# Linear attention on one core: the denominator moved into the four column groups of TensorE and spread afterwards

## The chip, the cores and the metric

One core of one Trainium2 chip runs the whole program. The metric is the device time of one execution in microseconds. A profile is one more execution, taken by the hardware profiler. Its "span" is about 1.7 us shorter than the time of the same execution.

## The reference, cut to what matters

```python
B, S, D = 1, 2048, 640;  H = 32; Dh = 20          # bf16 inputs
q, k, v = split_heads(x @ wqkv)
phi = lambda t: where(t > 0, t + 1, exp(t)) + 1e-6
pq, pk = phi(q), phi(k)
kv  = einsum("bhsd,bhse->bhde", pk, v)
z   = einsum("bhsd->bhd", pk)
num = einsum("bhqd,bhde->bhqe", pq, kv)
den = einsum("bhqd,bhd->bhq", pq, z)[..., None] + 1e-6   # one number per row and head
out = (num / den) merged over heads @ wo
```

There are only 32 denominators for each of the 2048 rows, but each divides 20 features.

## The kernel before

The kernel keeps `pq` transposed: 128 feature rows by 512 sequence rows, five such pieces (`c`) for each of four row blocks (`sbk`). The 128 feature rows of a piece are 32 heads times 4 features. Since `kv` and `wo` are folded into one matrix (`w2p`), the kernel divides `pq` by the denominator before the output matmul. The denominator therefore has to stand on all 128 feature rows. The kernel before gets this straight from TensorE: its weight block `zb` is 128 wide and repeats each head's column four times.

```python
def den(sbk, b):
    def mm(e):
        for c in range(NC_):                       # 5 matmuls of 128x512
            r = e.matmul(bank(b), zb[:, 128 * c:128 * c + 128],
                         pq[:, c * S + BK * sbk:c * S + BK * (sbk + 1)],
                         start=(c == 0), stop=(c == NC_ - 1))
        return r
    P.add("pe", mm, ...)
    i = sbk % 2
    P.add("act", lambda e: e.activation(lb[i], bank(b), ACTF.Ln, bias=eps[:, 0:1]), ...)
    P.add("act", lambda e: e.activation(rd[i], lb[i], ACTF.Exp, scale=-1.0), ...)   # 1/den

def normalize(sbk):                                # VectorE: pq *= rd, 5 times 128x512
    ...

# ... (program order of the second half; q = make one Q tile in the PSUM bank named)
den(0, 4); next_q(7); w2_group(2, 2); next_q(5); w2_group(3, 0); normalize(0)
next_q(6); w2_group(4, 2); next_q(7); w2_group(5, 0)
den(1, 4); w2_rows(); next_q(5); next_q(6); normalize(1)
while qi[0] < 15:
    next_q((7, 2, 3, 5, 6)[qi[0] % 5])             # one Q tile, the 15th: bank 6
next_q(0); next_q(1); den(2, 4)
next_q(2); normalize(2); next_q(3); next_q(5)
for st in range(2): out_tile(st)                   # output tile st uses banks 2*(st%4), +1
den(3, 6); normalize(3)
for st in range(2, NT): out_tile(st)
```

A Q tile is five 128x512 matmuls, an Exp on ScalarE (`eq`), and two operations on VectorE (`eq`, then `pq`, which is the last to read the bank). Each engine has its own list of instructions and waits on semaphores for the others.

Of the kernel before, what the change touches and what calls it, by code (L numbers as in the profile page):

```python
# [6 lines left out]
ACTF = mybir.ActivationFunctionType  # L7
ALU = mybir.AluOpType
BF16 = mybir.dt.bfloat16
F32 = mybir.dt.float32  # L10
# [72 lines left out]
def bass_standalone__linear_attn_block__prompt_kernel(nc, x, wqkv, wo, out):  # L83
    B, S, D = x.shape
    assert (B, S, D) == (1, 2048, 640)
    H, DH = 32, 20
    NC_ = D // 128
    NT = S // 128
    HALF = D // 2
    NSB = S // 512  # L90
    GW, NG = 120, 6
    gsz = [min(GW, D - GW * g) for g in range(NG)]
    BK = 512

    with contextlib.ExitStack() as ctx:
        es = ctx.enter_context

        def sb(name, cols, dt=BF16):
            return es(nc.sbuf_tensor(name, [128, cols], dt))
# [10 lines left out]
        pq = sb("pq", NC_ * S)  # L110
# [5 lines left out]
        za = [sb(f"za{j}", 2 * D, F32) for j in range(4)]  # L116
        zs = sb("zs", D, F32)
        zc = sb("zc", 8, F32)
        zb = sb("zb", NC_ * 128)
        hm = sb("hm", 128)  # L120
        bm = sb("bm", GW)
        ones = sb("ones", 8, F32)
        eps = sb("eps", 8, F32)
        zero = sb("zero", BK)
        lb = [sb(f"lb{j}", BK, F32) for j in range(2)]
        rd = [sb(f"rd{j}", BK) for j in range(2)]
        osb = [sb(f"osb{j}", D) for j in range(4)]
        ps = es(nc.psum_tensor("ps", [128, 8 * BK], F32))
        w2d = nc.dram_tensor("w2_rows", (D, D), BF16, kind="Internal").ap()

        P = Plan(nc, es)

        def bank(b, n=BK, off=0, parts=128):
            return ps[0:parts, BK * b + off:BK * b + off + n]
# [5 lines left out]
        def fold(ap, j=HALF):  # L140
            return ap.rearrange("p (g j) -> p g j", j=j)


        def pool_const():
            P.add("dve", lambda e: e.memset(zero[:, :], 0.0), writes=["zero"])
            P.add("dve", lambda e: e.memset(ones[:, :], 1.0), writes=["ones"])
            P.add("dve", lambda e: e.memset(eps[:, :], 1e-6), writes=["eps"])  # L147
            P.add("pool", lambda e: e.memset(wv[:, NC_ * D:], 0.0), writes=["wvpad"])
            P.add("pool", lambda e: e.memset(hm[:, :], 1.0), writes=["hm"])
            P.add("pool", lambda e: e.memset(bm[:, :], 1.0), writes=["bm"])  # L150
            for t, w, name in ((hm, 4, "hm"), (bm, DH, "bm")):
                n = t.shape[1] // w
                for lo in (True, False):
                    P.add("pool", lambda e, t=t, w=w, n=n, lo=lo: e.affine_select(
                        out=t[:, :].rearrange("p (a b) -> p a b", b=w),
                        in_=t[:, :].rearrange("p (a b) -> p a b", b=w),
                        pattern=[[-w if lo else w, n], [0, w]],
                        base=0 if lo else w - 1,
                        channel_multiplier=1 if lo else -1,
                        compare_op=ALU.is_ge, fill=0.0), reads=[name], writes=[name])  # L160

        XCH = [(0, 256), (256, 512), (512, 1024), (1024, 1536), (1536, 2048)]

# [158 lines left out]
        def z_finish(b):  # L322
            def mm(e):
                for c in range(NC_):
                    r = e.matmul(bank(b, 1, off=c), zs[:, 128 * c:128 * c + 128],
                                 ones[:, 0:1], start=True, stop=True)
                return r
            P.add("pe", mm, reads=["zs", "ones"], writes=[("bank", b)])
            P.add("dve", lambda e: e.tensor_copy(zc[:, 0:NC_], bank(b, NC_)),
                  reads=[("bank", b)], writes=["zc"])  # L330
            for c in range(NC_):
                P.add("dve", lambda e, c=c: e.tensor_scalar(
                    zb[:, 128 * c:128 * c + 128], hm[:, :], zc[:, c:c + 1], None, ALU.mult),
                    reads=["hm", "zc"], writes=[("zb", c)])

        def kv_group(b):
# [25 lines left out]
        def w2_group(g, b):  # L362
            n = gsz[g]
            for h in range(2):
                P.add("pe", lambda e, h=h: e.matmul(  # L365
                    bank(b + h, HALF, parts=n), kvt[0:n, GW * g:GW * g + n],
                    wog[0:n, g * D + HALF * h:g * D + HALF * (h + 1)], start=True, stop=True),
                    reads=[("kvt", 0 if g < 4 else g - 3), "wog", "wog5"],
                    writes=[("bank", b + h)])
            P.add("act", lambda e: e.copy(  # L370
                fold(w2g[0:n, g * D:(g + 1) * D]), two_banks(b, parts=n)),
                reads=[("bank", b), ("bank", b + 1)], writes=[("w2g", g)])

        def w2_rows():
            P.add("sp", lambda e: e.dma_start(
                w2d[0:5 * GW, :].rearrange("(g p) n -> p g n", p=GW),
                w2g[0:GW, 0:5 * D].rearrange("p (g n) -> p g n", n=D)),
                reads=[("w2g", g) for g in range(5)], writes=["w2d"], dma=True)
            P.add("sp", lambda e: e.dma_start(
                w2d[5 * GW:D, :], w2g[0:gsz[5], 5 * D:6 * D]),  # L380
                reads=[("w2g", 5)], writes=["w2d5"], dma=True)
            for c in range(NC_):
                P.add("sp", lambda e, c=c: e.dma_start(
                    w2p[:, c * D:(c + 1) * D],
                    w2d.rearrange("(h c j) n -> c h j n", c=NC_, j=4)[c]),
                    reads=["w2d", "w2d5"], writes=[("w2p", c)], dma=True)

        def den(sbk, b):
            def mm(e):
                for c in range(NC_):  # L390
                    r = e.matmul(bank(b), zb[:, 128 * c:128 * c + 128],  # L391
                                 pq[:, c * S + BK * sbk:c * S + BK * (sbk + 1)],
                                 start=(c == 0), stop=(c == NC_ - 1))
                return r
            P.add("pe", mm, reads=[("zb", c) for c in range(NC_)]
                  + [("pq", sbk, c) for c in range(NC_)], writes=[("bank", b)])
            i = sbk % 2
            P.add("act", lambda e: e.activation(lb[i][:, :], bank(b), ACTF.Ln, bias=eps[:, 0:1]),  # L398
                  reads=[("bank", b), "eps", "table"], writes=[("lb", i)])
            P.add("act", lambda e: e.activation(rd[i][:, :], lb[i][:, :], ACTF.Exp, scale=-1.0),  # L400
                  reads=[("lb", i)], writes=[("rd", i)])

        def normalize(sbk):
            i = sbk % 2
            for c in range(NC_):
                v = pq[:, c * S + BK * sbk:c * S + BK * (sbk + 1)]
                P.add("dve", lambda e, v=v: e.tensor_tensor(v, v, rd[i][:, :], ALU.mult),  # L407
                      reads=[("rd", i), ("pq", sbk, c)], writes=[("pq", sbk, c)])

        def out_tile(st):  # L410
            b = 2 * (st % 4)
            j = st % 4
            for h in range(2):
                def mm(e, h=h):
                    for c in range(NC_):
                        r = e.matmul(bank(b + h, HALF),  # L416
                                     pq[:, c * S + 128 * st:c * S + 128 * st + 128],
                                     w2p[:, c * D + HALF * h:c * D + HALF * (h + 1)],
                                     start=(c == 0), stop=(c == NC_ - 1))
                    return r  # L420
                P.add("pe", mm, reads=[("pq", st // 4, c) for c in range(NC_)]
                      + [("w2p", c) for c in range(NC_)], writes=[("bank", b + h)])
            P.add("act", lambda e: e.copy(osb[j][:, 0:HALF], bank(b, HALF)),  # L423
                  reads=[("bank", b)], writes=[("osb", j, 0)])
            P.add("dve", lambda e: e.tensor_copy(osb[j][:, HALF:D], bank(b + 1, HALF)),  # L425
                  reads=[("bank", b + 1)], writes=[("osb", j, 1)])
            P.add("sp", lambda e: e.dma_start(
                out[0, 128 * st:128 * st + 128, :], osb[j][:, :]),
                reads=[("osb", j, 0), ("osb", j, 1)], writes=[("out", st)], dma=True)
# [14 lines left out]
        def next_q(b):  # L444
            q_tile(*qs[qi[0]], b)
            qi[0] += 1
# [17 lines left out]
        next_q(6)  # L464
        w2_group(1, 0)
        den(0, 4)
        next_q(7)
        w2_group(2, 2)
        next_q(5)
        w2_group(3, 0)  # L470
        normalize(0)
# [3 lines left out]
        w2_group(5, 0)  # L475
        den(1, 4)
        w2_rows()
        next_q(5)
        next_q(6)
        normalize(1)  # L480
        while qi[0] < 15:
            next_q((7, 2, 3, 5, 6)[qi[0] % 5])
        next_q(0)
        next_q(1)
        den(2, 4)
        next_q(2)
        normalize(2)
        next_q(3)
        next_q(5)
        for st in range(2):  # L490
            out_tile(st)
        den(3, 6)
        normalize(3)
        for st in range(2, NT):
            out_tile(st)

        block = es(nc.Block())
# [51 lines left out]
```

## Time and profile before

| | before |
|---|---|
| time, median | 111.83 us |
| TensorE busy | 101.5 of 110.1 us |
| denominator matmuls | 4 x 5, 216 ns apart: 1.08 us a block |
| Ln and Exp of a block | 688 and 630 ns |
| waits of TensorE after 58 us | 1.75, 0.31 and about 0.25 us (the last worked out from starts, as a record is missing there) |

First the page: engine totals with shares of the span and instruction counts, the granted clock in 40 slices (9 is 90% or more), and the shares of the chain of waits by engine.

```profile
PE 101.5 (92%) x662; PEld 64.0 (58%) x668; DVE 66.9 (61%) x132; ACT 41.9 (38%) x73; POOL 5.9 (5%) x16
...
PEclk9999999999999999999999999999999999999999
...
PE 70%; DVE 15%; DMA 6%; ACT 5%; issue 1%
```

TensorE is busy for 92% of the span and makes 70% of the chain. So its matmul time counts, wherever it is not waiting. The groups view says what one instruction costs (count, then busy us and mean ns of one, then idle before it):

```profile
L391 PE MATMUL ps<-pq,zb 128*128 128x512 bf16 x19 | 4.8, 380 | 0.4 <-DVE pq L288 0.3
L398 ACT ACTIVATE lb<-ps,eps 128x512 f32<-128x512 f32 x4 | 2.8, 688 | 3.4 <-PE ps L391 3.4
L400 ACT ACTIVATE rd<-lb 128x512 bf16<-128x512 f32 x4 | 2.5, 630 | 0.1
L344 PE MATMUL ps<-pt,wv 128*40 128x40 bf16 x5 | 0.3, 182 | 0.0
```

A mean of 380 ns is the life of one matmul, not its price: the next one starts after 216 ns. One of the 20 denominator records is missing. TensorE's timeline in order of time shows the prices (start us, length us, line, count; a length runs from the first start to the last end):

```profile
64.21 1.25 PE L391 MATMUL ps<-pq,zb 128*128 128x512 bf16 x5
65.30 1.24 PE L275 MATMUL ps<-xT,wqp 128*128 128x512 bf16 x5
66.38 0.44 PE L365 MATMUL ps<-wog,kvt 120*120 120x320 bf16 x2
66.66 1.24 PE L275 MATMUL ps<-xT,wqp 128*128 128x512 bf16 x5
...
70.92 1.25 PE L391 MATMUL ps<-pq,zb 128*128 128x512 bf16 x5
72.00 2.32 PE L275 MATMUL ps<-xT,wqp 128*128 128x512 bf16 x9
76.08 3.41 PE L275 MATMUL ps<-xT,wqp 128*128 128x512 bf16 x15 [1.75 <-DVE pq L288]
79.33 1.24 PE L391 MATMUL ps<-pq,zb 128*128 128x512 bf16 x5
80.40 3.40 PE L275 MATMUL ps<-xT,wqp 128*128 128x512 bf16 x15
...
87.30 1.03 PE L391 MATMUL ps<-pq,zb 128*128 128x512 bf16 x4 [0.30 <-DVE pq L288]
88.17 8.04 PE L416 MATMUL ps<-w2p,pq 128*128 128x320 bf16 x58
```

From a block's first matmul to the next group's first are 1.07 to 1.09 us: that is what TensorE pays for a denominator. The record missing is the first of the last block, which therefore began at about 87.08 (87.30 less 0.216).

### The profile page before, as it was taken

What the parts mean: (1) busy time and instruction counts of PE and PEld (TensorE: products, weight loads), DVE (VectorE), ACT (ScalarE), POOL (GpSimd) and SP (SyncE); (2) the same over time, 40 slices, a digit from 0 to 9 for tenths busy, and PEclk for the clock granted to TensorE, in tenths of its full rate; (3) what the DMA queues carried; (4) which work ended last, traced back from release to release, by engine and by line L of the source; (5) the groups of instructions that cost most, each with busy time, mean ns of one, the idle gap of its engine ahead of it and who ended that gap; (6) DMA issues with size and microseconds to landing.
All of it is one profiled execution on the core that took longest, in us unless ns stands there. A gap on an engine that the chain in (4) does not pass through costs nothing.

```text
span 110.1 us, 1693 instructions
## 1 busy us (share of the span) xinstructions
PE 101.5 (92%) x662; PEld 64.0 (58%) x668; DVE 66.9 (61%) x132; ACT 41.9 (38%) x73; POOL 5.9 (5%) x16
## 2 busy tenths in 40 slices
PE   5969999999799999999999999993999799999990
PEld 2327777777477674676757745431446377777760
DVE  1004888998899899701137664969849837333331
ACT  3104555555500206202043379872575173333330
POOL 7100000750000000000000000000000000000000
PEclk9999999999999999999999999999999999999999
DMA  1999999999980000000000000082720032433333
GB/s 40 270 295 220 224 211 298 378 363 364 258 163 22 0 0 3 0 0 0 6 0 3 0 0 0 18 216 70 206 92 0 0 119 92 152 119 119 119 120 118
DMA packets 19497, 12.88 MB, mean 117 GB/s; under 512 B 10914, under 2 KB 19490, under 8 KB 19490
## 3 DMA queue, kind: packets, MB, share of 16 engines
q1 hardware_dynamic: 18178, 11.96, 39.4%
q10 hardware_dynamic: 1312, 0.82, 2.7%
q8 instruction: 5, 0.08, 0.3%
q14 instruction: 2, 0.02, 0.0%
HBM read 6.72 MB, written 3.44 MB: 92 GB/s over the span
## 4 chain that ended last, share of the span: by engine, by line
PE 70%; DVE 15%; DMA 6%; ACT 5%; issue 1%
PE ps L225 19%; PE ps L416 17%; PE ps L249 15%; PE ps L275 12%; DMA xT<-in_x_dram 6%; DVE pq L288 4%; PE ps L391 4%; DVE za L294 4%; ACT eq L283 2%; DVE eq L285 2%; DVE pq L407 2%; PE ps L344 1%; ACT lb L398 1%; PE ps L365 1%; ACT rd L400 1%
## 5 line engine op out<-in xcount | busy, mean ns | idle before, releaser
L275 PE MATMUL ps<-xT,wqp 128*128 128x512 bf16 x95 | 23.0, 379 | 2.0 <-DVE pq L288 1.8
L249 PE MATMUL ps<-pk,xn 128*128 128x320 bf16 x160 | 22.4, 299 | 0.8 <-DVE pk L240 0.7
L225 PE MATMUL ps<-wk,xT 128*128 128x320 bf16 x160 | 21.9, 299 | 1.1 <-DMA xT<-in_x_dram 1.1
L416 PE MATMUL ps<-w2p,pq 128*128 128x320 bf16 x160 | 22.2, 299 | 0.3 <-DVE pq L288 0.3
L249 PEld LDWEIGHTS ps<-pk,xn 128*128 128x128 bf16 x160 | 15.5, 98 | 7.9 <-DVE pk L240 1.0
L225 PEld LDWEIGHTS ps<-wk,xT 128*128 128x128 bf16 x160 | 15.6, 98 | 7.5 <-issue 1.5
L283 ACT ACTIVATE eq<-ps 128x512 bf16<-128x512 f32 x20 | 11.9, 595 | 21.2 <-PE ps L275 20.7
L416 PEld LDWEIGHTS ps<-w2p,pq 128*128 128x128 bf16 x160 | 15.6, 98 | 7.0 <-DVE pq L288 0.6
L235 ACT ACTIVATE ek<-ps 128x640 bf16<-128x640 f32 x16 | 11.3, 704 | 15.7 <-PE ps L225 15.7
L275 PEld LDWEIGHTS ps<-xT,wqp 128*128 128x128 bf16 x100 | 9.6, 98 | 12.2 <-DVE pq L288 2.2
L288 DVE SCALAR_TENSOR_TENSOR pq<-ps,eq 128x512 bf16<-128x512 f32 x20 | 13.8, 692 | 0.7
L285 DVE TENSOR_SCALAR eq<-eq 128x512 bf16<-128x512 bf16 x20 | 5.8, 290 | 12.8 <-ACT eq L283 12.6
L240 DVE SCALAR_TENSOR_TENSOR pk<-ps,ek 128x640 bf16<-128x640 f32 x16 | 13.2, 824 | 0.6
L425 DVE CAST osb<-ps 128x320 bf16<-128x320 f32 x16 | 7.7, 489 | 9.6 <-PE ps L416 9.5
L237 DVE TENSOR_SCALAR ek<-ek 128x640 bf16<-128x640 bf16 x16 | 6.1, 380 | 10.5 <-ACT ek L235 10.4
L423 ACT CAST osb<-ps 128x320 bf16<-128x320 f32 x16 | 6.8, 425 | 12.6 <-PE ps L416 12.5
L407 DVE TENSOR_TENSOR pq<-pq,rd 128x512 bf16<-128x512 bf16 x20 | 7.0, 417 | 2.0 <-ACT rd L400 2.0
L216 PE MATMUL ps<-zero 128*128 128x512 bf16 x16 | 5.2, 494 | 1.3 <-DVE eps L147 1.3
L261 ACT CAST pt<-ps 128x320 bf16<-128x320 f32 x6 | 2.2, 434 | 9.7 <-PE ps L249 9.7
L294 DVE TENSOR_TENSOR za<-pk 128x1280 f32<-128x1280 bf16 x4 | 5.7, 1483 | 0.0
L391 PE MATMUL ps<-pq,zb 128*128 128x512 bf16 x19 | 4.8, 380 | 0.4 <-DVE pq L288 0.3
L208 POOL COPY wqp<-wqn 128x640 bf16<-128x640 bf16 x5 | 3.6, 756 | 16.9 <-DMA wqn<-in_wqkv_dram 16.9
(30 smaller groups left out, 36.1 us busy)
## 6 DMA issues: line engine op xcount, KB each, us to landing
xn<-in_x_dram SPq DMA_DIRECT2D x4, 640.0 KB, 9.7
out_dram<-osb SPq DMA_DIRECT2D x16, 160.0 KB, 1.8
wk<-in_wqkv_dram ACTq DMA_DIRECT2D x2, 400.0 KB, 5.0
wqn<-in_wqkv_dram SPq DMA_DIRECT2D x1, 800.0 KB, 5.2
wv<-in_wqkv_dram SPq DMA_DIRECT2D x1, 800.0 KB, 14.3
w2p<-w_rows SPq DMA_DIRECT2D x5, 160.0 KB, 2.7
wog<-in_wo_dram SPq DMA_DIRECT2D x1, 750.0 KB, 14.8
w_rows<-w2g SPq DMA_DIRECT2D x1, 750.0 KB, 5.3
```

Source lines behind the costliest of these rows:

```text
L225: r = e.matmul(bank(b + h, HALF), xT[:, c * S + 128 * st:c * S + 128 * st + 128], wk[:, c * D + HALF * h:c * D + HALF * (h + 1)], start=(c ...
L235: P.add("act", lambda e: e.activation(fold(t[:, :]), two_banks(b), ACTF.Exp), reads=banks + ["table"], writes=[("ek", st % 3)])
L240: P.add("dve", lambda e: e.scalar_tensor_tensor(fold(pk[:, st * D:(st + 1) * D]), two_banks(b), 0.0, fold(t[:, :]), ALU.max, ALU.add), rea ...
L249: r = e.matmul(bank(d, HALF), xn[:, st * D + 128 * d:st * D + 128 * d + 128], pk[:, st * D + HALF * h:st * D + HALF * (h + 1)], start=(st ...
L275: r = e.matmul(bank(b), wqp[:, d * D + 128 * c:d * D + 128 * c + 128], xT[:, d * S + BK * sbk:d * S + BK * (sbk + 1)], start=(d == 0), sto ...
L283: P.add("act", lambda e: e.activation(t[:, :], bank(b), ACTF.Exp), reads=[("bank", b), "table"], writes=[("eq", i)])
L285: P.add("dve", lambda e: e.tensor_scalar(t[:, :], t[:, :], 1.0, 1e-6, ALU.min, ALU.add), reads=[("eq", i)], writes=[("eq", i)])
L288: P.add("dve", lambda e: e.scalar_tensor_tensor(pq[:, c * S + BK * sbk:c * S + BK * (sbk + 1)], bank(b), 0.0, t[:, :], ALU.max, ALU.add), ...
L294: P.add("dve", lambda e: e.tensor_tensor(d_ap, a, b, ALU.add), reads=ra + rb, writes=[dst])
L391: r = e.matmul(bank(b), zb[:, 128 * c:128 * c + 128], pq[:, c * S + BK * sbk:c * S + BK * (sbk + 1)], start=(c == 0), stop=(c == NC_ - 1))
L407: P.add("dve", lambda e, v=v: e.tensor_tensor(v, v, rd[i][:, :], ALU.mult), reads=[("rd", i), ("pq", sbk, c)], writes=[("pq", sbk, c)])
L416: r = e.matmul(bank(b + h, HALF), pq[:, c * S + 128 * st:c * S + 128 * st + 128], w2p[:, c * D + HALF * h:c * D + HALF * (h + 1)], start=( ...
```

## The change

Its intent: compute each denominator once, not four times. The weights `zb` become 32 wide. The 512 rows of a block are cut into four pieces of 128, and each piece goes to its own column group of the array (output partitions 0-31, 32-63, 64-95, 96-127), so that the four can run side by side. The sums then fill 128 partitions by 128 columns, a quarter of the columns for Ln and Exp. Four matmuls with a 0/1 mask `em` spread the inverse to the 128 feature rows, and ScalarE copies the result to `rd`.

```diff
-        zb = sb("zb", NC_ * 128)
-        hm = sb("hm", 128)
+        zb = sb("zb", NC_ * 32)
+        em = sb("em", 4 * 128)          # four 0/1 masks, made by GpSimd at the start
+        hm = sb("hm", 32)
 ... (building of the masks cut)
         def den(sbk, b):
             def mm(e):
                 for c in range(NC_):
-                    r = e.matmul(bank(b), zb[:, 128 * c:128 * c + 128],
-                                 pq[:, c * S + BK * sbk:c * S + BK * (sbk + 1)],
-                                 start=(c == 0), stop=(c == NC_ - 1))
+                    for k in range(4):
+                        r = e.matmul(
+                            ps[32 * k:32 * k + 32, BK * b:BK * b + 128],
+                            zb[:, 32 * c:32 * c + 32],
+                            pq[:, c * S + BK * sbk + 128 * k:c * S + BK * sbk + 128 * k + 128],
+                            start=(c == 0), stop=(c == NC_ - 1))
                 return r
+        def den_act(sbk, b):              # Ln and Exp on 128 columns -> rdc
+            ...
+        def den_spread(sbk, b):
+            def mm(e):
+                for k in range(4):
+                    r = e.matmul(bank(b, 128, off=128 * k), em[:, 128 * k:128 * k + 128],
+                                 rdc[i][:, :], start=True, stop=True)
+                return r
+            P.add("pe", mm, reads=["em", ("rdc", i)], writes=[("bank", b)])
+            P.add("act", lambda e: e.copy(rd[i][:, :], bank(b)), ...)
 ... (order: each den is followed by den_act; den_spread comes one or two tiles later)
         den(2, 4)
+        den_act(2, 4)
         next_q(2)
+        next_q(3)
+        den_spread(2, 4)
         normalize(2)
-        next_q(3)
         next_q(5)
         for st in range(2):
             out_tile(st)
         den(3, 6)
+        den_act(3, 6)
+        out_tile(2)
+        den_spread(3, 6)
         normalize(3)
-        for st in range(2, NT):
+        for st in range(3, NT):
             out_tile(st)
```

More of the change, by code (lines that the diff above doesn't have):

```diff
@@ L124, in bass_standalone__linear_attn_block__prompt_kernel @@
         zero = sb("zero", BK)
-        lb = [sb(f"lb{j}", BK, F32) for j in range(2)]
+        lb = [sb(f"lb{j}", 128, F32) for j in range(2)]
+        rdc = [sb(f"rdc{j}", 128) for j in range(2)]
         rd = [sb(f"rd{j}", BK) for j in range(2)]
@@ L150, in pool_const, with band @@
             P.add("pool", lambda e: e.memset(bm[:, :], 1.0), writes=["bm"])
-            for t, w, name in ((hm, 4, "hm"), (bm, DH, "bm")):
-                n = t.shape[1] // w
-                for lo in (True, False):
-                    P.add("pool", lambda e, t=t, w=w, n=n, lo=lo: e.affine_select(
-                        out=t[:, :].rearrange("p (a b) -> p a b", b=w),
-                        in_=t[:, :].rearrange("p (a b) -> p a b", b=w),
-                        pattern=[[-w if lo else w, n], [0, w]],
-                        base=0 if lo else w - 1,
-                        channel_multiplier=1 if lo else -1,
-                        compare_op=ALU.is_ge, fill=0.0), reads=[name], writes=[name])
+            P.add("pool", lambda e: e.memset(em[:, :], 1.0), writes=["em"])
+            def band(t, pat, base, mult, name):
+                v = t.rearrange("p (a b) -> p a b", b=pat[1][1])
+                P.add("pool", lambda e: e.affine_select(
+                    out=v, in_=v, pattern=pat, base=base, channel_multiplier=mult,
+                    compare_op=ALU.is_ge, fill=0.0), reads=[name], writes=[name])
+            band(hm[:, :], [[-4, 32], [0, 1]], 0, 1, "hm")
+            band(hm[:, :], [[4, 32], [0, 1]], 3, -1, "hm")
+            for k in range(4):
+                m = em[:, 128 * k:128 * k + 128]
+                band(m, [[-1, 32], [0, 4]], -32 * k, 1, "em")
+                band(m, [[1, 32], [0, 4]], 32 * k, -1, "em")
+            for lo in (True, False):
+                band(bm[:, :], [[-DH if lo else DH, NG], [0, DH]],
+                     0 if lo else DH - 1, 1 if lo else -1, "bm")
         XCH = [(0, 256), (256, 512), (512, 1024), (1024, 1536), (1536, 2048)]
@@ L332, in z_finish @@
                 P.add("dve", lambda e, c=c: e.tensor_scalar(
-                    zb[:, 128 * c:128 * c + 128], hm[:, :], zc[:, c:c + 1], None, ALU.mult),
+                    zb[:, 32 * c:32 * c + 32], hm[:, :], zc[:, c:c + 1], None, ALU.mult),
                     reads=["hm", "zc"], writes=[("zb", c)])
@@ L396, in den @@
                   + [("pq", sbk, c) for c in range(NC_)], writes=[("bank", b)])
+        def den_act(sbk, b):
             i = sbk % 2
-            P.add("act", lambda e: e.activation(lb[i][:, :], bank(b), ACTF.Ln, bias=eps[:, 0:1]),
+            P.add("act", lambda e: e.activation(lb[i][:, :], bank(b, 128), ACTF.Ln, bias=eps[:, 0:1]),
                   reads=[("bank", b), "eps", "table"], writes=[("lb", i)])
-            P.add("act", lambda e: e.activation(rd[i][:, :], lb[i][:, :], ACTF.Exp, scale=-1.0),
-                  reads=[("lb", i)], writes=[("rd", i)])
+            P.add("act", lambda e: e.activation(rdc[i][:, :], lb[i][:, :], ACTF.Exp, scale=-1.0),
+                  reads=[("lb", i)], writes=[("rdc", i)])
+        def den_spread(sbk, b):
+            i = sbk % 2
+            def mm(e):
+                for k in range(4):
+                    r = e.matmul(bank(b, 128, off=128 * k), em[:, 128 * k:128 * k + 128],
+                                 rdc[i][:, :], start=True, stop=True)
+                return r
+            P.add("pe", mm, reads=["em", ("rdc", i)], writes=[("bank", b)])
+            P.add("act", lambda e: e.copy(rd[i][:, :], bank(b)),
+                  reads=[("bank", b)], writes=[("rd", i)])
         def normalize(sbk):
@@ L466, in bass_standalone__linear_attn_block__prompt_kernel @@
         den(0, 4)
+        den_act(0, 4)
         next_q(7)
         w2_group(2, 2)
+        den_spread(0, 4)
         next_q(5)
@@ L477, in bass_standalone__linear_attn_block__prompt_kernel @@
         w2_rows()
+        den_act(1, 4)
         next_q(5)
         next_q(6)
+        den_spread(1, 4)
         normalize(1)
```

## The prediction

> **What bounds it now.** TensorE: 101.5 of 110.1 us busy (page, engine totals), full clock in every slice, and 70% of the chain of waits. The denominator matmuls are 4% of that chain. In the chain's time order four blocks of five 128x512 matmuls take 1.25, 1.20, 1.09 and about 1.25 us (87.07 to 88.33, one record missing); 216 ns each, about 1.08 us streaming. TensorE really waits at only three places from 58 us on (its timeline): 1.75 us before 76.08 (a Q tile reuses the bank of the Q tile before, so it waits for ScalarE and VectorE), 0.31 before 86.15 and about 0.25 before 87.07 (both for VectorE's pq).
>
> **Removed.** 20 streams of 512 columns become 80 of 128 in four column groups. Groups view: 128x40 weight-plus-matmul pairs of the kv step follow each other at about 30 ns (five span 0.30, one lasts 0.18), 128x120 ones at 53 ns. So a block is 20 x 30 = 0.6 us if the groups overlap and issue limits, 20 x 53 = 1.06 us if they don't. The Trainium skill ("TensorE: Matmul & The Clock Gate", What's actually happening) gives about 25 ns as the smallest start-to-start, which fits the 30 ns here. I take 0.75 us: 0.33 saved per block, 1.3 us in all.
>
> **Added by the tile mode.** The skill ("TensorEngine Tiling (Array Packing)", Key Properties) says that changing tiling mode drains TensorE. In this trace the 40*40 matmuls start 0.31 us after the last 512-column one (216 ns usual) and the next full matmul 0.23 us after the last of them (136 usual): about 0.09 us per switch. Seven exposed switches: 0.6 us.
>
> **ScalarE saves nothing.** Ln 688 and Exp 630 ns at 512 columns shrink to about 360 and 310 (slope 0.85 ns per column, from Exp at 512 and 640 columns: 595 and 704), but a 512-column copy of about 600 ns is added.
>
> **Spread.** Four 128-column matmuls, 0.21 us a block. Block 0: on TensorE's critical stretch, +0.2. Block 1: falls into the 1.75 us wait, free. Block 2: free, because VectorE decides when denominator 3 may start (Q tiles 17, 18, 19 and the normalize: about 6.4 us after denominator 2 in both orders). Block 3: +0.2 and a new wait: it writes bank 6, which output tile 3 needs next, so TensorE waits for the spread's completion and the 0.6 us copy: about +0.8 us. Nothing else is there for it to do.
>
> **Small.** The five zb products on 32 columns instead of 128 shorten a wait of at most 0.2 us: -0.1. The masks add some 4 us to GpSimd at the start, where it idles 17 us: free.
>
> **Sum.** -1.3 + 0.6 + 0.2 + 0.2 + 0.8 - 0.1 = +0.4 us. Predicted 112.2 us, range 111.2 to 113.9. Chances: faster by over 2% 0.02, within 2% 0.90, slower by over 2% 0.08.
>
> **What would show it.** Denominator block: first to last start plus one, 0.6 to 0.9 us. Full matmul after it about 0.1 us late. TensorE idle of 0.7 to 0.9 us before output tile 3, ended by ScalarE's rd copy. The wait before the 15th Q tile stays, ended by VectorE pq, a little shorter. Denominator 3 still released by VectorE pq. Output stage still about 136 ns per matmul.
>
> **What would make it wrong.** Column groups that don't overlap, or weight loads of 32 columns that aren't hidden behind them: a block of 1.1 us or more, +1.3 us or more in all. Switches that cost nothing: -0.6. A later VectorE order that frees den 3 sooner. The spread finding its inverse not ready (I expect over 0.4 us of slack everywhere).

One reference in it needs a correction: the figure of 25 ns stands on the page named, but in the section after the one named, "Wait — 56ns, not 53.3ns?".

## The result, and the profile after

The changed kernel takes 110.52 us (median of 4, 110.34 to 110.94); the kernel before in the same rounds takes 111.82. The ratio is 0.9886, interval 0.9854 to 0.9919. The change gains 1.3 us where I had forecast a loss of 0.4; the time lies below the range I gave.

The page after, the same lines as before:

```profile
PE 100.1 (92%) x738; PEld 64.2 (59%) x744; DVE 66.7 (61%) x132; ACT 41.4 (38%) x77; POOL 10.2 (9%) x25
...
PE 72%; DVE 13%; DMA 6%; ACT 5%; issue 1%
```

TensorE lost 1.4 us of busy time although it has 76 more matmul records. The groups view after:

```profile
L405 PE MATMUL ps<-pq,zb 128*32 128x128 bf16 x80 | 1.9, 221 | 0.3 <-DVE pq L300 0.3
L416 ACT ACTIVATE lb<-ps,eps 128x128 f32<-128x128 f32 x4 | 1.5, 370 | 1.1 <-PE ps L405 1.1
L418 ACT ACTIVATE rdc<-lb 128x128 bf16<-128x128 f32 x4 | 1.2, 310 | 0.1
L430 ACT CAST rd<-ps 128x512 bf16<-128x512 f32 x4 | 2.3, 587 | 0.5 <-PE ps L426 0.5
```

And TensorE's timeline after:

```profile
64.64 0.46 PE L405 MATMUL ps<-pq,zb 128*32 128x128 bf16 x20
65.04 1.25 PE L287 MATMUL ps<-xT,wqp 128*128 128x512 bf16 x5
66.13 0.44 PE L377 MATMUL ps<-wog,kvt 120*120 120x320 bf16 x2
66.40 0.39 PE L426 MATMUL ps<-rdc,em 128*128 128x128 bf16 x4
66.62 1.24 PE L287 MATMUL ps<-xT,wqp 128*128 128x512 bf16 x5
...
70.88 0.46 PE L405 MATMUL ps<-pq,zb 128*32 128x128 bf16 x20
71.28 2.33 PE L287 MATMUL ps<-xT,wqp 128*128 128x512 bf16 x10
...
75.36 3.41 PE L287 MATMUL ps<-xT,wqp 128*128 128x512 bf16 x14 [1.52 <-DVE pq L300]
78.70 0.46 PE L405 MATMUL ps<-pq,zb 128*32 128x128 bf16 x20
79.09 2.33 PE L287 MATMUL ps<-xT,wqp 128*128 128x512 bf16 x10
...
85.77 0.46 PE L405 MATMUL ps<-pq,zb 128*32 128x128 bf16 x20 [0.32 <-DVE pq L300]
86.16 1.53 PE L446 MATMUL ps<-w2p,pq 128*128 128x320 bf16 x10
87.53 0.39 PE L426 MATMUL ps<-rdc,em 128*128 128x128 bf16 x4
88.59 7.64 PE L446 MATMUL ps<-w2p,pq 128*128 128x320 bf16 x55 [0.68 <-ACT rd L430]
```

A block of 20 narrow matmuls lasts 0.46 us, of which the last matmul's own life is 0.22: first to last start are 0.24 us, 12.6 ns per matmul on average. The next matmul starts 0.39 to 0.40 us after the block's first. Before it was 1.08.

Putting the same milestones of the two traces side by side gives a ledger. "Step" is by how much the difference changes from one line to the next.

| TensorE starts | before | after | difference | step, and what it is |
|---|---|---|---|---|
| first k matmul | 7.49 | 8.04 | +0.55 | load of x in this execution |
| denominator 0 | 64.21 | 64.64 | +0.43 | -0.12, shorter zb products |
| Q tile after it | 65.30 | 65.04 | -0.26 | -0.69, denominator 0 |
| Q tile after spread 0 | 66.66 | 66.62 | -0.04 | +0.22, spread 0 |
| Q tile after denominator 1 | 72.00 | 71.28 | -0.72 | -0.68, denominator 1 |
| 15th Q tile | 76.08 | 75.36 | -0.72 | 0, spread 1 |
| Q tile after denominator 2 | 80.40 | 79.09 | -1.31 | -0.59, denominator 2 |
| denominator 3 | 87.08 | 85.77 | -1.31 | 0, spread 2 |
| output tile 2 | 88.17 | 86.16 | -2.01 | -0.70, denominator 3 |
| output tile 3 | 89.53 | 88.59 | -0.94 | +1.07, spread 3 and its wait |

(Output tile 3 before is worked out: ten matmuls of 136 ns after output tile 2.) Leaving out the first line, which is a longer load of x in the profiled execution (the slowest of its four, 110.94 us), the change gains 1.5 us: the four denominator blocks give 2.66, the zb products 0.12, and spreads 0 and 3 take back 1.29. The load was issued at 0.81 us in both traces and took 7.09 us against 6.55. It does not come with the change: in the nine other traces of kernels with the changed denominator the first k matmul starts at 7.30 to 7.84 us.

### The profile page after: what moved, and what is told of

Its sections match the earlier page's. It is cut to its first block, busy times and chain, and to the rows that moved or that the text cites. A ratio compares the mean times of both kernels' runs of the same rounds, so it can differ in the third digit from the quotient of the medians.

```text
span 109.2 us, 1857 instructions
## 1 busy us (share of the span) xinstructions
PE 100.1 (92%) x738; PEld 64.2 (59%) x744; DVE 66.7 (61%) x132; ACT 41.4 (38%) x77; POOL 10.2 (9%) x25
## 4 chain that ended last, share of the span: by engine, by line
PE 72%; DVE 13%; DMA 6%; ACT 5%; issue 1%
PE ps L237 19%; PE ps L446 18%; PE ps L261 15%; PE ps L287 15%; DMA xT<-in_x_dram 6%; DVE za L306 4%; DVE pq L300 3%; ACT eq L295 3%; DVE pq L437 2%; PE ps L405 2%; PE ps L356 1%; DVE eq L297 1%; ACT rd L430 1%; PE ps L337 1%; PE ps L377 1%
## 5 line engine op out<-in xcount | busy, mean ns | idle before, releaser
L249 DVE TENSOR_SCALAR ek<-ek 128x640 bf16<-128x640 bf16 x16 | 5.4, 339 | 11.5 <-ACT ek L247 11.3
L220 POOL COPY wqp<-wqn 128x640 bf16<-128x640 bf16 x5 | 3.6, 756 | 12.7 <-DMA wqn<-in_wqkv_dram 12.7
L306 DVE TENSOR_TENSOR za<-za 128x1280 f32<-128x1280 f32 x3 | 4.4, 1487 | 0.0
```

What stands on the lines that cost most here:

```text
L306: P.add("dve", lambda e: e.tensor_tensor(d_ap, a, b, ALU.add), reads=ra + rb, writes=[dst])
```

## The experiments

Ten kernels ran; all gave correct results and all ran in the fast state, but for the single look, whose one run has no state. They were timed in three sessions on different chips. The kernel before took 111.93 us beside the four edits called order, halved, doubled and bank; 111.80 beside the one group and the next three on waits (order on VectorE, bank 7, kernel before repaired); and 111.98 beside the last normalize and the single look. So 0.2 us between medians of two sessions says little. Unless said otherwise an edit is made to the changed kernel (110.5 us).

### Do the groups run side by side? All into one group

The cost of a block was the step of my prediction that failed, so it comes first. Theory A: the column groups overlap. Rival B: a matmul with 32 weight columns is quick in itself. This kernel makes the same 80 loads and matmuls of the same shape, all in the first group (with the loop over `k` outside, so one column range after the other).

```diff
-                        ps[32 * k:32 * k + 32, BK * b:BK * b + 128],
+                        ps[0:32, BK * b + 128 * k:BK * b + 128 * k + 128],
 # Ln, Exp on 32x512; the spread is one matmul: em[0:32, 0:128] by rdc[0:32, 0:512]
```

> The same 80 weight loads and matmuls of 32 weight columns by 128 columns, but all into one column group (partitions 0 to 31, four column ranges); Ln and Exp then run on 32x512 and one matmul of 32 rows spreads the inverse. Results stay right. Theory A (the groups run side by side, each with 56 ns between its own matmuls): with one group nothing overlaps, 19*56 = 1.06 us from first to last start, about +0.8 us a block; with Ln and Exp longer by 0.3 us each, +3.3 us over the changed kernel, some 113.8 us or a little more. Theory B (what is quick is the narrow matmul, groups or no groups): starts 12 to 26 ns apart, block no longer than 0.5 us, under +1 us.

It took 114.24 us (113.91 to 114.42), ratio 1.02 to the kernel before. TensorE's timeline of this kernel, first block:

```profile
64.46 1.29 PE L405 MATMUL ps<-pq,zb 128*32 128x128 bf16 x20
65.68 1.25 PE L287 MATMUL ps<-xT,wqp 128*128 128x512 bf16 x5
```

1.29 less the last one's 0.22 is 1.07 us for 19 steps: 56 ns each. B is refuted, A holds. A block of narrow matmuls without the groups costs 1.22 us (64.46 to 65.68), more than the five full-width matmuls that it replaces.

### Does the order matter? Group by group

```diff
-                for c in range(NC_):
-                    for k in range(4):
+                for k in range(4):
+                    for c in range(NC_):
```

> The 80 narrow denominator matmuls in the other loop order: all five of one column group, then the next group; same count, same results. Theory A (successive matmuls overlap because they go to different column groups): inside a group they follow at 53 ns, so a block takes about 17*53+3*13 = 0.94 us from first to last start instead of 0.24, about +0.7 us for each of four blocks, all on the critical chain: about +2.8 us over the changed kernel, some 113.2 us. Theory B (a 32-column matmul of 128 columns is simply quick to issue, whatever its group): block unchanged at 0.24 us, time unchanged at about 110.5 us.

111.31 us (111.09 to 111.54): neither. The first block in TensorE's timeline:

```profile
64.16 0.67 PE L405 MATMUL ps<-pq,zb 128*32 128x128 bf16 x20
64.76 1.25 PE L287 MATMUL ps<-xT,wqp 128*128 128x512 bf16 x5
```

First to last start took 0.45 us (0.67 less 0.22) in every block, not 0.94 and not 0.24. Both theories took for granted that matmuls start in program order. If each group worked off its own five matmuls 56 ns apart, and TensorE reached the next group's matmuls while the earlier group was still busy, the last group would begin late but not after the others. That became theory C, and the next kernel tested it.

### Who starts when? One source line for each group

Same instructions in the same order as the kernel just before, but the five matmuls of each group are written on a line of their own (407, 409, 411, 413 for groups 0 to 3), so the trace names the group.

> The kernel with the group-by-group loop order (111.3 us), with each column group's matmuls on a source line of its own, so that the trace tells the groups apart. Theory C (each group works off its own matmuls 56 ns apart, and TensorE sends later matmuls to a free group before earlier ones of a busy group have started): matmuls of the second group start before the last of the first, and the last starts about 0.46 us after the first. Theory D (starts keep program order; matmuls of one group follow at about 24 ns): the four groups' starts do not interleave. Time unchanged at 111.3 us.

111.17 us. TensorE's timeline of the first block:

```profile
64.05 0.28 PE L407 MATMUL ps<-pq,zb 128*32 128x128 bf16 x2
64.12 0.23 PE L409 MATMUL ps<-pq,zb 128*32 128x128 bf16 x1
64.17 0.22 PE L407 MATMUL ps<-pq,zb 128*32 128x128 bf16 x1
64.19 0.22 PE L409 MATMUL ps<-pq,zb 128*32 128x128 bf16 x1
64.19 0.23 PE L411 MATMUL ps<-pq,zb 128*32 128x128 bf16 x1
...
64.28 0.22 PE L407 MATMUL ps<-pq,zb 128*32 128x128 bf16 x1
64.30 0.22 PE L409 MATMUL ps<-pq,zb 128*32 128x128 bf16 x1
...
64.44 0.28 PE L413 MATMUL ps<-pq,zb 128*32 128x128 bf16 x2
```

In the program all five of line 407 come before the first of line 409. On the chip the first of 409 starts at 64.12 and the last of 407 at 64.28. So C holds and D falls: each group has its own sequence with 55 to 56 ns between starts after a first step of 66, and TensorE sends matmuls to a free group past those that wait for a busy one. The raw starts of this block, in ns from its first, are 0, 66, 122, 178, 233 for group 0; 72, 138, 194, 250, 306 for group 1; 144, 211, 267, 323, 378 for group 2; and 217, 283, 338, 394, 450 for group 3. This sending ahead has a limit: each group begins only 6 ns after the second start of the group before it (72 after 66, 144 after 138, 217 after 211). These three late starts are why the block still takes 0.45 us; no run shows what sets the limit. In the order of the changed kernel (column groups inside), four start 3 to 4 ns apart and the next four 45 to 57 ns after the last of these. That is why its block takes 4 x 56 ns plus little.

### Is it the 128 columns or an issue limit? Columns halved

```diff
-                for c in range(NC_):
-                    for k in range(4):
+                for o, c, k in [(o, c, k) for o in (0, 64) for c in range(NC_) for k in range(4)]:
-    ... 128 columns from 128 * k
+    ... 64 columns from 128 * k + o
```

> Each narrow matmul is split into two of 64 columns: 160 a block instead of 80, same columns in all. Theory A (the 12.6 ns between starts is four groups streaming 128 columns each at the same time, 53/4 = 13.3 ns): half the columns, 6 to 7 ns between starts, block and time unchanged, about 110.5 us. Theory B (12.6 ns or more is a floor for issuing a weight load and a matmul): 12 ns stays, block 0.25 us longer, +1.0 us, some 111.5 us; if the floor is the 25 ns that the skill's page states, +0.5 us a block and more.

110.45 us (110.23 to 110.96): unchanged. The last block in TensorE's timeline:

```profile
85.25 0.49 PE L405 MATMUL ps<-pq,zb 128*32 128x64 bf16 x40
85.68 1.53 PE L446 MATMUL ps<-w2p,pq 128*128 128x320 bf16 x10
```

Twice as many matmuls in a block that costs 0.43 us instead of 0.39. First to last start are 0.29 us in the raw records for 39 steps, 7.5 ns on average. So 12.6 ns was no floor for issuing, nor was the 25 ns of the page that the prediction names. Theory A holds; the 0.04 us more shows that it is not entirely free.

### What does the change of mode cost? Each block twice

```diff
-                for c in range(NC_):
-                    for k in range(4):
+                for rep in range(2):
+                    for c in range(NC_):
+                        for k in range(4):
```

> Each denominator block is issued twice in a row (the second overwrites the first with the same sums): 40 narrow matmuls between one entry into the column mode and one exit. Theory A (a block's cost of 0.49 us is 0.25 us of matmuls at 12.6 ns plus about 0.25 us once for entry and exit): +0.25 us for each of four blocks, +1.0 us, some 111.5 us; 40 matmuls from first to last start about 0.49 us. Theory B (the whole cost comes with the matmuls, the change of mode is free): +0.4 to 0.5 us a block, +1.6 to 2.0 us, some 112.3 us.

111.44 us (111.17 to 111.57), 0.9 above the changed kernel: theory A. In its timeline:

```profile
85.95 0.74 PE L406 MATMUL ps<-pq,zb 128*32 128x128 bf16 x40 [0.32 <-DVE pq L300]
86.63 1.53 PE L447 MATMUL ps<-w2p,pq 128*128 128x320 bf16 x10
```

Twenty more matmuls cost 0.28 or 0.29 us (0.74 against 0.46; 0.68 against 0.39 to the next matmul). So of the 0.39 us that a block costs, 0.28 are its matmuls and 0.11 is paid once, at the exit. An entry costs about as much where it shows: before denominator 2 the last Q matmul starts at 78.39 in the trace and the first narrow one at 78.70, 0.31 us later, where 0.216 is usual. It is not any change of shape that costs this: around the last spread of the bank experiment below, full-width matmuls of 128 columns follow the 320-column ones after the usual 136 ns and are followed after 56 ns (raw starts).

### Is the last wait the bank? The last spread into bank 1

```diff
-        den_spread(3, 6)
+        den_spread(3, 1)
```

> Only the last spread writes bank 1 (next needed by output tile 4) instead of bank 6 (next needed by output tile 3). Theory A (the 0.7 us wait of TensorE before output tile 3 is the bank, held until ScalarE has copied the spread): the wait is gone, about -0.75 us against the changed kernel, some 109.7 us. Theory B (the wait is for something else that the last block brings, such as the inverse itself): unchanged, about 110.5 us.

109.50 us (109.44 to 109.64), ratio 0.9782 (0.9762 to 0.9802): faster than the kernel before, by 2.2%; whether by over 2% is not settled, as the interval reaches 0.9802. The timeline:

```profile
86.83 0.39 PE L426 MATMUL ps<-rdc,em 128*128 128x128 bf16 x4
87.06 8.18 PE L446 MATMUL ps<-w2p,pq 128*128 128x320 bf16 x59
```

The output matmuls follow the spread after 0.23 us instead of 1.06: 0.83 us gained. The wait was the bank. The rest of the 1.0 us between the medians (of different rounds) is within the spread of the changed kernel's own runs (110.34 to 110.94).

### The waits that the change did not make

The three remaining kernels ask what is left of TensorE's waits, and end in a kernel that beats both. First, on top of bank 1, the normalize of block 2 moves behind the last Q tile on VectorE.

```diff
-        normalize(2)
         next_q(5)
+        normalize(2)
```

> On top of the kernel with the last spread in bank 1: the normalize of block 2 comes after the last Q tile on VectorE instead of before it. Theory A (denominator 3 waits only because VectorE does 1.7 us of normalize before the pq of the last Q tile): the 0.32 us wait of TensorE goes, -0.3 us, some 109.2 us. Theory B (that wait is set by the Q tile itself, or returns as a wait of an output tile): unchanged at 109.5 us.

109.14 us (109.05 to 109.54), and TensorE's timeline shows no wait before denominator 3. Theory A. The trace says so; the times alone do not, since the ratios of the two kernels to the kernel before, 0.9764 and 0.9782, lie within each other's intervals. Then the 15th Q tile goes to bank 7:

```diff
-            next_q((7, 2, 3, 5, 6)[qi[0] % 5])
+            next_q(7)
```

> As the kernel with both the bank 1 and the order, and the 15th Q tile goes to bank 7, long free, instead of bank 6, held by the Q tile before. The 1.5 us wait of TensorE there goes; in its place the first output tile should wait for the folded weights from memory, which land about 80.6 us in, against a start at 81.9 us now: about -1.0 to -1.3 us, some 108.0 us. If the 1.5 us wait was VectorE's work and not the bank, it comes back before denominator 2 or 3 and the gain is under 0.5 us.

108.43 us (108.26 to 108.47): a gain of 0.7, not 1.0 to 1.3, and no wait where I expected one. The timeline says why:

```profile
73.16 3.40 PE L287 MATMUL ps<-xT,wqp 128*128 128x512 bf16 x14
77.44 0.46 PE L405 MATMUL ps<-pq,zb 128*32 128x128 bf16 x20 [0.88 <-DVE pq L300]
```

The 1.5 us wait for the bank is gone, but 0.88 came back before denominator 2: VectorE does 1.7 us of normalize for block 1 before the 15th Q tile's `pq`. Moving that normalize too:

```diff
-        normalize(1)
         while qi[0] < 15:
             next_q(7)
         next_q(0)
         next_q(1)
+        normalize(1)
         den(2, 4)
```

> On top of the kernel with bank 1, bank 7 and the late normalize of block 2: the normalize of block 1 comes after the 17th Q tile instead of before the 15th. TensorE's 0.88 us wait before denominator 2 (for the 15th Q tile's pq, behind 1.7 us of normalize) should go; the folded weights land at about 80.9 us and the first output tile starts at 81.3 now, so I expect only 0.4 to 0.5 us of it as gain: some 108.0 us, with a wait for the weights before the first output tile. If the wait was not this normalize: unchanged, 108.4 us.

108.18 us (107.97 to 108.25), ratio 0.9657 (0.9644 to 0.9671): the fastest of all. The wait before denominator 2 is gone, and the first output tile now waits 0.55 us, as I expected. The size of the gain is uncertain: 0.25 us between the two medians, which come from different chips, but 0.43 us if each kernel is taken against the kernel before of its own rounds (3.80 and 3.37 us faster). I expected 0.4 to 0.5.

```profile
80.86 2.88 PE L446 MATMUL ps<-w2p,pq 128*128 128x320 bf16 x20 [0.55 <-DVE eq L297]
```

The name in the bracket is VectorE's `eq`, which an output matmul does not read. The last load of the folded weights was issued at 77.9 us and such a load lands after 2.9 us (median), at about 80.8. In the raw trace the last of them lands at 80.77 and the first weight load of an output matmul starts at 80.83. So I read the wait as one for the weights; no run takes it away to prove it.

Last, the kernel before with the two repairs that do not belong to the change (bank 7, normalize of block 2 behind the last Q tile):

> The kernel before, with the same two repairs that do not belong to the change (bank 7 for the 15th Q tile, normalize of block 2 after the last Q tile). If these waits have nothing to do with the change, it gains about as much, -1.5 to -1.9 us, some 110.1 us, and the change plus its bank repair is then worth about 2 us on top of it, as it was without them (111.9 against 109.5).

110.49 us (110.42 to 110.73), ratio 0.9878: a gain of 1.3, somewhat less than I expected. Its wait before denominator 2 is 1.11 us, the same VectorE work as above. Against 108.43 the change with its own bank repair is worth 2.1 us here, against 2.4 without the two repairs (111.93 and 109.50). So most of what the change gains does not depend on these two waits.

## Why the prediction was wrong

The place of every effect was forecast correctly, and so were the sizes, but for one and for the number of mode changes that show.

- **TensorE bounds it, denominator blocks count in full.** Right: four blocks shortened the chain by 0.69, 0.68, 0.59 and 0.70 us.
- **"20 x 30 = 0.6 us if the groups overlap and issue limits ... I take 0.75 us: 0.33 saved per block."** This is the step that failed. The matmuls of a block cost 0.28 us (the doubled block), so 1.08 - 0.28 = 0.80 us is saved before the change of mode. Four times the 0.47 us that I missed is 1.9 us, which is the whole distance from the forecast of +0.4 to the ledger's -1.5; by the medians the prediction was 1.7 us too slow (112.2 against 110.52). The mistake was one of reading. The 128x40 matmuls of the trace, 30 ns apart on average (raw starts 42, 25, 25 and 25 ns apart), all wrote the same output partitions, so their spacing tells what one place in the array allows. I took it for an issue limit of the whole engine, and a floor of about 25 ns from the Trainium skill ("TensorE: Matmul & The Clock Gate", section "Wait — 56ns, not 53.3ns?") seemed to confirm it. The same page, Part 3, gives about 4 ns between starts in different tiles, which is what this trace shows (3 to 4 ns); I had the right figure at hand and used the other. My own numbers would have given the right sum: with the groups side by side, each works off five matmuls 53 ns apart, 5 x 53 = 0.27 us, against the 0.28 measured.
- **A change of mode costs about 0.09 us.** Right in size: 0.11 at an exit, 0.09 at the entry that shows. Five showed, not seven: denominator 0 waited for zb and denominator 3 for VectorE anyway, and denominator 1 follows a 40*40 matmul, after which the kernel before paid as well.
- **ScalarE saves nothing.** Right: Ln 370 and Exp 310 ns against the 360 and 310 forecast, and a copy of 587 ns; ScalarE's busy time went from 41.9 to 41.4 us.
- **Spreads 1 and 2 are free, 0 costs 0.2.** Right: steps of 0, 0 and +0.22 in the ledger. VectorE still released denominator 3, in both traces 6.68 us after the matmul that follows denominator 2.
- **The last spread costs 0.2 and a wait of 0.8 for bank 6.** Right: +1.07 in the ledger, and the bank experiment took 0.83 away.
- **zb products -0.1; masks free.** Right: -0.12, and GpSimd, 4.3 us busier, still idles 12.7 us before its next work.

## What to carry to other kernels

Before you cost concurrent tiles, ask whether the spacing that you read in a trace is between instructions in the same tile or in different ones: here the two differ by more than ten times (56 against 3 to 4 ns). The first kind counts once for each matmul of one group (5 x 56 = 0.28 us here), the second once for each matmul of all groups (20 x 4 = 0.08 us). Here the longer of the two sums was what a block's matmuls cost. Narrow weights alone gain nothing; the gain comes from giving independent work to all four column groups, with the groups in the inner loop. When a new intermediate needs a PSUM bank, choose one whose next user is far away: one number in this change was worth 0.8 us of the 2.4 that it then gains.

## What the Trainium skill lacked or had wrong

- "TensorE: Matmul & The Clock Gate", section "Wait — 56ns, not 53.3ns?": the floor of about 25 ns between starts is stated without saying that it holds within a tile. Across column groups starts were 3 to 4 ns apart, and 40 matmuls of 64 columns averaged 7.5 ns. Within one group 128 columns gave 56 ns, which agrees with the page.
- The same page, Part 3, The mechanism: it says that matmuls start and end strictly in program order. With column groups they start out of it: the first of group 1 began 72 ns into the block, the third of group 0, earlier in the program, at 122 ns. (Ends are modelled in these profiles, so nothing is said of them.)
- The same section's list of what overlaps says that a weight load overlaps matmuls in flight only when the row group differs. Here 80 loads that use all rows stayed hidden behind matmuls of other column groups, and even within a single group the spacing was 56 ns with a load of 97 ns for every matmul. The section's own text also allows a load into a background weight buffer, which may be what happened here; its list leaves that out.
- "TensorEngine Tiling (Array Packing)", Key Properties: it says that a change of mode drains TensorE, with no figure. Here it was 0.09 us on entry and 0.11 us on exit.
- The same page, Restrictions, says that column tiling disables the fast weight load. No run tells whether it was off here: loads of 32 columns are recorded at 97 ns, as long as the 98 of 128 columns, but they overlapped, so that even one group's matmuls started 56 ns apart.
